# Spreading the first projections, and DVE units before V is complete, in a fused attention kernel

## The chip, the cores and the metric

The kernel runs on one core of one Trainium2 chip. The time is the device time of one execution in microseconds (us), and the median of several executions is compared. The engines are named as in the profile: PE (matmuls), PEld (weight loads, beside PE), DVE (vector work), ACT (activation functions), POOL (general purpose), SP (issues DMAs). Each engine works through its own instructions in order and waits on semaphores that the others raise.

## The reference

Two attention layers run over the same input of 2,048 tokens by 640 features, with 32 heads of 20 features. Layer A is full softmax attention; layer B attends to eight earlier tokens, two apart. A gate per token mixes them.

```python
q, k, v = qkv[0], qkv[1], qkv[2]
scores = jnp.einsum("bhqd,bhkd->bhqk", q, k) * scale      # A: every token to every token
p = _softmax(scores, axis=-1)
o = jnp.einsum("bhqk,bhkd->bhqd", p, v)                   # then reshaped and @ wo
...
idx = pos[:, None] - off[None, :]                         # B: off = 0, 2, ... 14
attn = _softmax(logits, axis=-1)
...
return g * a + (1 - g) * b                                # g = sigmoid(x . gate_w)
```

All inputs and the output are bfloat16. By far the most work is the exponential of layer A: 32 heads x 2,048 x 2,048 scores.

## The kernel before

**Units, groups and tiles.** Scores of layer A are cut into units: one head, 128 keys, 512 queries. Four heads and 512 queries make a group (`GROUPS`, L34: 4 query chunks x 8 head quads = 32 groups); a group has 16 key blocks x 4 heads = 64 units, so 2,048 in all. The order of groups starts with head quad 0 for query chunks 0 and 1, then the other seven quads of chunk 0, then those of chunk 1, and so on. Two or three units that are scored together make a tile. `next_tile` (L1463) picks them, `qk` (L1502) writes their score matmuls into one of two PSUM buffers of three banks each, and `exp` (L1535) writes one ACT instruction (L1538) over the tile, 1,024 columns for two units and 1,536 for three. The third bank of each buffer is also a bank for side work, together with one bank more, so a tile of three units needs that bank to be free.

**Units on DVE.** A tile of two units can take along a third unit, a ride, that DVE evaluates instead of ACT. DVE turns the scores into 16-bit integers whose bits, read as bfloat16, approximate the exponential (`uD`, L1528). Three shifted copies (`eD`, L797) with weighted copies of V (`vS`, on POOL, L789) smooth the approximation. So a unit on ACT costs one V-product matmul and a unit on DVE four (`pv`, L1547; matmuls at L1583). Rides are opened by `wanted` (L1389), a key block of four heads at a time, and always the last key block of a group that is still unread; an opening needs an idle DVE by the planner's reckoning. There are two thresholds: `DIDLE2` opens at any time, and the laxer `DIDLE` only once the last V block is projected and layer B's work is on schedule.

**Side work.** All else goes between the score rounds as generators in pieces: K (`gen_kd`, L582), Q (`gen_qd`) and V (`gen_v`, L717) projections, the gate, layer B (`gen_b`, `gen_bproj`), norms and the output fold (`gen_fold`). A projection piece is four matmuls of 32 columns of the array beside each other over 512 (V: 320) columns of data at L557; five pieces make a bank, which DVE then copies out. K is projected in five chunks of features, V in two halves (head quads 0 to 3, 4 to 7) of 16 key blocks. If a V product asks for a V block that is not projected yet, `run_until` (L1211) emits side work at once until it is.

**The order of work.** The kernel's Python code is itself a planner. It keeps a modelled clock per engine and appends instructions to each engine's list; the order is fixed when the program is built. After each score round and exponential, `spend` (L1614) emits side work up to a limit after the modelled end of the last exponential but one (`SLACK`), and where nothing is ready, a filler (L1590, matmuls at L1604): a matmul with no use but to keep PE working. Every parameter of these choices (`SLACK`, ride thresholds, priorities, look-ahead, filler share) is set from the table `PLAN`, keyed by the tile's number (read at L1693).

Of the kernel before, what the change touches and what calls it, by code (L numbers as in the profile page):

```python
# [21 lines left out]
KBN = S // P  # L22
# [26 lines left out]

PLAN = {  # L50
    0: ((0.34, 0.64), 0.37, 6.3, 2.5, 0.51, -1.0, -0.1, 11.8, 4.5, 7.2, 0.52, 0.47, 4.4, 1.86, 0.0, 0.85, 2, 0.0),
    10: ((0.34, 0.64), 0.37, 6.3, 2.5, -0.17, -1.0, -0.1, 13.02, 4.5, 7.2, 0.52, 0.47, 4.4, 1.86, 0.0, 0.85, 2, 0.0),
    20: ((0.34, 0.64), 0.21, 6.3, 6.6, -0.17, -1.0, -0.1, 13.02, 4.5, 8.28, 0.52, 0.47, 4.4, 1.86, 0.0, 0.85, 2, 0.0),
    30: ((0.28, 0.52), 0.35, 2.5, 6.6, 0.49, -1.55, -0.55, 9.24, 6.7, 7.2, 0.53, 0.57, 4.23, 4.64, 0.02, 0.85, 2, 1),
    50: ((0.28, 0.52), 0.35, 2.5, 6.6, 0.49, -1.55, -0.55, 9.24, 6.7, 7.2, 0.25, 0.57, 4.23, 4.64, -0.13, 0.85, 2, 1),
    60: ((0.28, 0.52), 0.35, 2.5, 6.6, 0.49, -1.55, -0.55, 9.24, 6.7, 7.2, 0.53, 0.57, 4.23, 4.28, 0.16, 0.85, 2, 1),
    70: ((0.28, 0.52), 0.1, 2.5, 6.6, 0.49, 0.2, -0.55, 9.24, 6.7, 7.2, 0.5, 0.57, 4.23, 4.64, 0.02, 0.85, 2, 1),
    80: ((0.28, 0.52), 0.34, 2.5, 5.5, 0.49, -1.55, -0.62, 9.24, 7.0, 7.2, 0.53, 0.57, 4.55, 4.64, 0.02, 0.85, 2, 1),
    90: ((0.28, 0.52), 0.3, 2.5, 6.6, 0.49, -1.55, -0.55, 9.24, 6.7, 7.8, 0.5, 0.57, 4.23, 4.64, 0.02, 0.85, 2, 1),
    110: ((0.28, 0.52), 0.3, 2.5, 6.6, 0.49, -1.55, -0.55, 8.84, 6.7, 7.8, 0.5, 0.57, 4.23, 4.64, 0.02, 0.85, 2, 0),  # L60
    120: ((0.28, 0.52), 0.3, 5.5, 6.6, 0.49, -1.34, -0.55, 8.84, 6.7, 7.8, 0.5, 0.57, 4.23, 4.64, 0.05, 0.85, 2, 0),
    130: ((0.28, 0.52), 0.19, 5.5, 6.3, 0.49, -0.24, -0.53, 9.24, 6.7, 11.3, 0.53, 0.57, 4.23, 4.93, -0.13, 0.89, 2, -3),
    140: ((0.28, 0.52), 0.3, 2.5, 2.5, 0.87, -1.55, -0.55, 8.84, 6.7, 7.8, 0.5, 0.57, 3.8, 4.64, 0.02, 0.85, 2, 0),
    170: ((0.28, 0.52), 0.3, 2.5, 2.5, 0.87, -1.28, -0.55, 8.42, 6.7, 7.8, 0.5, 0.54, 3.8, 4.64, 0.02, 0.85, 2, 0),
    180: ((0.28, 0.52), 0.39, 6.6, 2.5, 0.87, -1.55, -0.65, 10.03, 6.7, 7.8, 0.5, 0.57, 3.8, 3.83, 0.02, 0.87, 2, -3),
    190: ((0.28, 0.52), 0.19, 2.5, 2.5, 0.7, -1.55, -0.55, 7.32, 6.7, 7.8, 0.5, 0.5, 3.8, 2.96, 0.02, 0.85, 2, -3),
    200: ((0.23, 0.54), 0.35, 2.5, 2.5, 0.87, -1.55, -0.55, 7.13, 6.7, 7.71, 0.5, 0.57, 3.46, 4.13, 0.02, 0.86, 2, -3),
    210: ((0.28, 0.52), 0.3, 2.5, 2.5, 0.9, -1.55, -0.6, 7.13, 6.7, 7.71, 0.5, 0.49, 3.46, 4.64, 0.02, 0.85, 2, -3),
    220: ((0.32, 0.54), 0.3, 2.5, 2.5, 1.16, -1.55, -0.6, 7.13, 6.7, 7.71, 0.5, 0.49, 3.46, 4.64, 0.02, 0.85, 2, -3),
    230: ((0.28, 0.52), 0.3, 2.5, 2.5, 0.9, -1.55, -0.6, 7.61, 6.7, 7.71, 0.5, 0.49, 3.46, 4.64, 0.02, 0.81, 2, -3),  # L70
    250: ((0.28, 0.52), 0.3, 2.5, 2.5, 0.9, -1.48, -0.27, 7.13, 4.5, 7.32, 0.5, 0.36, 3.46, 4.64, 0.02, 0.66, 2, -3),
    280: ((0.28, 0.52), 0.3, 2.5, 2.5, 0.9, -1.48, -0.27, 7.13, 4.5, 7.32, 0.5, 0.41, 3.46, 4.64, 0.02, 0.66, 2, -3),
    290: ((0.28, 0.52), 0.3, 2.5, 5.5, 0.9, -1.6, -0.6, 7.13, 6.7, 10.69, 0.5, 0.49, 3, 4.64, 0.02, 0.67, 2, -3),
    310: ((0.28, 0.52), 0.3, 2.5, 5.5, 0.9, -1.6, -0.6, 14.73, 6.7, 10.69, 0.5, 0.49, 5.63, 4.64, 0.02, 0.67, 2, -3),
    320: ((0.28, 0.52), 0.3, 2.5, 5.5, 1.26, -1.56, -0.6, 7.13, 6.7, 10.69, 0.5, 0.53, 3, 4.64, 0.02, 0.67, 2, -3),
    330: ((0.27, 0.53), 0.26, 2.5, 5.5, 0.58, -1.6, -0.6, 7.13, 4.5, 10.54, 0.5, 0.49, 3, 4.64, 0.11, 0.67, 2, -3),
    340: ((0.27, 0.53), 0.3, 2.5, 5.5, 0.9, -1.5, -0.6, 7.13, 7.0, 10.54, 0.41, 0.49, 3.17, 4.64, 0.2, 0.67, 2, -3),
    350: ((0.27, 0.53), 0.26, 1.0, 5.5, 0.58, -1.6, -0.6, 7.13, 4.5, 10.54, 0.5, 0.49, 3, 4.64, 0.02, 0.69, 1, -3),
    360: ((0.28, 0.52), 0.37, 2.5, 5.5, 1.26, -1.56, -0.6, 7.13, 6.7, 10.69, 0.5, 0.53, 5.91, 4.64, 0.02, 0.67, 2, -3),
    400: ((0.28, 0.52), 0.37, 2.5, 5.5, 1.26, -1.56, -0.6, 7.13, 4.5, 10.69, 0.5, 0.53, 5.91, 4.64, 0.02, 0.67, 2, -3),  # L80
    410: ((0.23, 0.54), 0.22, 2.5, 6.3, 1.26, -1.56, -0.6, 7.13, 6.7, 10.69, 0.5, 0.53, 5.35, 4.64, 0.02, 0.6, 2, -3),
    420: ((0.24, 0.49), 0.3, 2.5, 5.5, 1.26, -1.56, -0.59, 7.13, 6.7, 10.69, 0.5, 0.53, 6.0, 4.64, 0.02, 0.67, 2, -3),
    430: ((0.24, 0.49), 0.3, 2.5, 5.5, 1.26, -1.56, -0.59, 7.13, 6.7, 10.69, 0.51, 0.53, 6.0, 4.64, 0.02, 0.67, 2, -3),
    450: ((0.26, 0.56), 0.3, 2.5, 5.5, 1.26, -1.56, -0.59, 7.13, 6.7, 10.69, 0.5, 0.53, 6.0, 4.64, 0.02, 0.67, 2, 0),
    480: ((0.26, 0.56), 0.3, 2.5, 5.5, 1.26, -1.4, -0.59, 9.8, 6.7, 10.69, 0.5, 0.53, 6.0, 4.64, 0.02, 0.67, 2, 0),
    500: ((0.26, 0.56), 0.3, 2.5, 5.5, 1.26, -1.56, -0.59, 7.13, 6.7, 10.69, 0.5, 0.53, 6.0, 4.64, 0.02, 0.76, 2, -1.5),
    510: ((0.26, 0.56), 0.3, 2.5, 5.5, 1.26, -1.56, -0.09, 7.13, 6.7, 10.69, 0.5, 0.53, 6.0, 4.64, 0.02, 0.76, 2, -3),
    530: ((0.21, 0.59), 0.3, 2.5, 6.6, 1.26, -1.56, -0.43, 7.13, 6.7, 10.69, 0.5, 0.53, 6.0, 4.64, -0.23, 0.76, 2, -3),
    540: ((0.21, 0.58), 0.3, 6.6, 5.5, 1.26, -0.43, -0.09, 7.13, 6.7, 10.33, 0.5, 0.53, 6.0, 4.64, 0.08, 0.76, 2, -3),
    550: ((0.21, 0.59), 0.3, 2.5, 6.6, 1.26, -1.56, -0.43, 7.13, 6.7, 11.31, 0.49, 0.53, 6.0, 4.64, -0.36, 0.76, 2, -3),  # L90
    570: ((0.2, 0.61), 0.3, 2.5, 6.6, 1.26, -1.56, -0.43, 7.13, 6.7, 10.69, 0.5, 0.53, 6.0, 4.64, -0.23, 0.76, 2, -3),
    580: ((0.2, 0.56), 0.3, 2.5, 5.5, 1.26, -1.56, 0.15, 9.66, 6.7, 8.54, 0.49, 0.48, 6.0, 4.64, -0.36, 0.76, 2, -3),
    590: ((0.2, 0.56), 0.26, 2.5, 1.0, 1.26, -1.56, 0.15, 7.13, 6.7, 11.31, 0.49, 0.31, 6.0, 4.64, -0.36, 0.76, 2, -3),
    600: ((0.28, 0.45), 0.32, 2.5, 5.5, 1.26, -0.49, -0.43, 10.79, 5.5, 10.35, 0.57, 0.53, 6.0, 4.64, -0.33, 0.66, 2, -3),
    630: ((0.28, 0.45), 0.32, 2.5, 5.5, 0.96, -0.49, -0.43, 10.79, 5.5, 10.35, 0.65, 0.53, 6.0, 4.64, -0.33, 0.66, 2, -3),
    660: ((0.28, 0.45), 0.32, 2.5, 5.5, 0.96, -0.1, -0.27, 10.79, 5.5, 10.35, 0.65, 0.53, 6.0, 4.64, -0.33, 0.66, 2, -3),
    670: ((0.28, 0.5), 0.32, 2.5, 5.5, 1.11, -0.49, -0.43, 10.79, 6.2, 10.35, 0.65, 0.55, 6.5, 4.81, -0.39, 0.62, 2, -3),
    690: ((0.3, 0.64), 0.32, 2.5, 2.5, 0.49, -1.0, -0.1, 11.8, 5.5, 7.2, 0.52, 0.47, 4.4, 4.0, 0.0, 0.85, 2, 0.0),
    700: ((0.42, 0.48), 0.32, 6.3, 5.5, 0.76, -0.49, -0.43, 10.79, 5.5, 10.35, 0.65, 0.53, 6.0, 4.64, -0.33, 0.63, 2, -3),
}  # L100
WEIGHTS = (1.0, 0.83984375, 0.70703125, 0.59375)
UOFF = 15992.765
# [217 lines left out]
def _build(ctx, nc, A_x, A_wqkv, A_wo, B_wqkv, B_wo, gate_w, out):  # L320
# [3 lines left out]
    sch = _Sched(nc, ctx)  # L324
# [242 lines left out]
    done = {}  # L567
# [13 lines left out]

    def gen_kd():  # L582
        for f in range(CN):
            m = P if f < CN - 1 else D - 4 * DH - P * (CN - 1)
            for tcc in range(4):
                b = yield from bank()
# [51 lines left out]
        done[("q", 1)] = True  # L638

    qkeys = {}  # L640
    BATCH = (0, 1, 2, 3, 4)

    def gen_qd():
# [71 lines left out]
                batch = []  # L715

    def gen_v(half):  # L717
        for kb in range(NV0 if half == 0 else 0, KBN):
            b = yield from bank()
            mms = [(side[b][:, 0:320], xT[:, c, kb * P:(kb + 1) * P],  # L720
                    kvw[:, WV_OFF + c * D + half * 320:WV_OFF + c * D + half * 320 + 320]) for c in range(CN)]
            yield from mm_group(b, mms, ["WvA"] + XT(kb // 4), mmc(320))
            yield ("dve",)
            o = _ap(vA, (kb * NQ + 4 * half) * 4 * DV + 1, [[DV, 16], [1, DH]])
            i = sap(b, 0, [[DH, 16], [1, DH]])
            t = T("dve", dvc(320), lambda e, o=o, i=i: e.tensor_copy(o, i), reads=[("side", b), "vAones"],
                  writes=[("vA", kb, half)])
            release(b, t)
            done[("v", kb, half)] = True
# [89 lines left out]
    bdone = [0.0]  # L819
# [317 lines left out]
    clock = [0.0]  # L1137
# [239 lines left out]
    DIDLE = -1.0  # L1377
    D0 = 26.0

    BT0 = 230.0  # L1380
    BT1 = 860.0
    BALL = 172.0
    DIDLE2 = -0.1
# [5 lines left out]
    def wanted(js):  # L1389
# [7 lines left out]

        if not dopen:
            if ulock[len(dquads) % 2] or len(dquads) > cur["pv"] + 1 or now < D0 or not (
                    idle >= DIDLE2 or idle >= DIDLE and done.get(("v", KBN - 1, 1)) and bdone[0] >= (now - BT0) / (BT1 - BT0) * BALL):  # L1400
                return None
            t_end = sch.avail["act"]
            for g in range(cur["g"], min(NG, cur["g"] + 2)):
# [374 lines left out]
```

## Time and profile before

| | before |
|---|---|
| device time, median of 3 | 836.64 us (835.95 to 837.18) |
| span of the profiled execution | 835.4 us |
| PE, DVE, ACT busy | 789.3, 683.7, 803.9 us |
| exponentials on ACT | 735 (479 of two units, 255 of three, 1 of one) |
| units on DVE | 324 of 2,048 |
| granted PE clock, mean | 0.998 |

A profile line of a group gives the source line, the engine, the operation, what it writes and reads, its shape and how often; then the busy time, the mean of one in nanoseconds, and the time that the engine sat idle just before, with the instruction that ended the wait. Instructions that overlap on an engine are counted once in the busy time. In a timeline line the first two numbers are the start and the length of a run of equal instructions.

### The profile page before, as it was taken

To read this page: it belongs to the slowest core of one execution; us is meant where nothing else is said; L and a number is where in the kernel's file an instruction comes from. 1 tells how busy PE (TensorE), PEld (TensorE's weight loads), DVE (VectorE), ACT (ScalarE), POOL (GpSimd) and SP (SyncE) were. 2 spreads that over 40 slices of the span, in tenths; PEclk is the share of its full clock that TensorE was granted. 3 is DMA by queue.
4 is the path that set the end of the run, shared out by engine and by line. 5 is a ranking of instruction groups with operands and counts; after the bars stand their busy time and mean duration, and the time that the engine had idled before them with its cause. 6 is when DMAs were issued, how large, how long until landed. Compare 5 with 4: busy or idle time off the path is not lost.

```text
span 835.4 us, 29602 instructions
## 1 busy us (share of the span) xinstructions
PE 789.3 (94%) x12599; PEld 289.9 (35%) x12601; DVE 683.7 (82%) x1205; ACT 803.9 (96%) x767; POOL 138.7 (17%) x180
## 2 busy tenths in 40 slices
PE   8999999999999899989998999999999999998997
PEld 4333323334333332333233333333333333333223
DVE  7567888889888887978797988798898898887873
ACT  4999999999999999999999999999999999999994
POOL 5013013431111111011111011111102111101110
PEclk9999999999999999999999999999999999999999
DMA  9112112200111110011001011110011001101100
GB/s 313 30 37 44 33 25 45 73 13 19 29 37 29 29 30 20 7 42 32 20 18 41 18 20 29 36 42 9 5 39 30 10 20 25 38 6 31 32 6 34
DMA packets 45016, 29.15 MB, mean 35 GB/s; under 512 B 27204, under 2 KB 43684, under 8 KB 44884
## 3 DMA queue, kind: packets, MB, share of 16 engines
q1 hardware_dynamic: 44596, 26.92, 12.4%
q8 instruction: 100, 1.64, 0.8%
q10 hardware_dynamic: 288, 0.33, 0.1%
q14 instruction: 32, 0.26, 0.1%
HBM read 11.94 MB, written 2.62 MB: 17 GB/s over the span
## 4 chain that ended last, share of the span: by engine, by line
PE 54%; ACT 30%; issue 10%; DVE 5%; DVEq 0%; ACTq 0%
ACT ebuf L1538 30%; PE score L1515 17%; PE obank L1583 13%; PE side L557 13%; PE score L557 5%; PE obank L1604 2%; DVE uD L1528 1%; PE side L1604 1%; DVE eD L797 1%; PE obank L459 1%; PE score L1230 1%; PE side L885 1%; DVE stage L869 0%; PE score L1604 0%; DVE stage L970 0%
## 5 line engine op out<-in xcount | busy, mean ns | idle before, releaser
L1538 ACT ACTIVATE ebuf<-score 128x1024 bf16<-128x1024 f32 (+1 forms) x735 | 792.6, 1237 | 11.6 <-PE score L1515 9.7
L1515 PE MATMUL score<-qT,kT 32*128 32x512 bf16 x2048 | 291.9, 384 | 31.6 <-ACT ebuf L1538 20.6
L1528 DVE TENSOR_SCALAR uD<-score 128x512 int16<-128x512 f32 x324 | 217.2, 683 | 38.4 <-PE score L1515 36.1
L797 DVE TENSOR_SCALAR eD<-uD 128x2048 int16<-128x2048 int16 x243 | 168.1, 722 | 7.9 <-PE obank L1583 7.2
L1515 PEld LDWEIGHTS score<-qT,kT 32*128 32x128 bf16 x2048 | 75.1, 91 | 282.7 <-ACT ebuf L1538 137.6
L1583 PE MATMUL obank<-ebuf,vA 128*21 128x512 bf16 x1724 | 161.3, 385 | 2.2 <-ACT ebuf L1538 1.8
L789 POOL TENSOR_TENSOR vS<-vA,vw 128x252 bf16<-128x252 bf16 x81 | 61.0, 757 | 291.5 <-PE obank L1583 256.3
L557 PE MATMUL side<-xT,kvw 128*32 128x256 bf16 (+1 forms) x2530 | 103.0, 281 | 3.1 <-DVE qkvB L853 1.4
L1583 PE MATMUL obank<-eD,vS 128*21 128x512 bf16 x972 | 84.1, 382 | 0.0
L557 PEld LDWEIGHTS side<-xT,kvw 128*32 128x32 bf16 x2530 | 59.3, 96 | 37.9 <-issue 22.0
L764 POOL TENSOR_TENSOR rcp<-rcp,gA 128x16 f32<-128x16 f32 x31 | 11.3, 365 | 351.9 <-DVE rcp L762 351.9
L1583 PEld LDWEIGHTS obank<-ebuf,vA 128*21 128x21 bf16 x1724 | 38.6, 89 | 82.3 <-issue 69.5
L970 DVE TENSOR_TENSOR stage<-qkvB,repB 128x1280 bf16<-128x1280 bf16 x64 | 52.9, 856 | 0.7 <-DMA repB<-eB 0.7
L869 DVE TENSOR_TENSOR stage<-qkvB 128x1280 bf16<-128x1280 bf16 x64 | 51.4, 830 | 0.1
L853 DVE CAST qkvB<-side 128x512 bf16<-128x512 f32 (+1 forms) x72 | 41.9, 591 | 10.5 <-PE side L557 10.5
L557 PE MATMUL side<-stage,ident 128*32 128x512 bf16 (+1 forms) x736 | 47.4, 345 | 1.2 <-DVE uD L744 0.5
L1604 PE MATMUL obank<-xT,zero 128*32 128x512 bf16 x444 | 37.9, 385 | 0.0
L770 POOL TENSOR_TENSOR oN<-oTt,rcp 128x512 bf16<-128x512 f32 x31 | 33.0, 1065 | 2.4
L1583 PE MATMUL obank<-uD,vA 128*21 128x512 bf16 x324 | 31.7, 382 | 0.0
L758 DVE STREAM_TRANSPOSE oTt<-obank 128x512 f32<-128x512 f32 x32 | 22.7, 709 | 9.0 <-PE obank L1583 8.9
L1583 PEld LDWEIGHTS obank<-eD,vS 128*21 128x21 bf16 x972 | 24.0, 92 | 17.4 <-issue 4.1
L557 PE MATMUL side<-woA_d,oTd 128*32 128x128 bf16 (+1 forms) x580 | 28.8, 293 | 0.0
(173 smaller groups left out, 555.5 us busy)
## 6 DMA issues: line engine op xcount, KB each, us to landing
repB<-eB SPq DMA_DIRECT2D x128, 32.0 KB
WqP<-in_A_wqkv_dram SPq DMA_DIRECT2D x16, 160.0 KB
stage<-in_B_wqkv_dram SPq DMA_DIRECT2D x1, 2400.0 KB
oTd<-oN SPq DMA_DIRECT2D x108, 20.0 KB
qT<-dst SPq DMA_DIRECT2D x104, 20.0 KB
out_dram<-outsb SPq DMA_DIRECT2D x12, 160.0 KB
kvw<-in_A_wqkv_dram SPq DMA_DIRECT2D x2, 800.0 KB
oTd<-in_A_x_dram SPq DMA_DIRECT2D x2, 640.0 KB
```

The lines of the kernel that those rows point to most:

```text
L557: ins = e.matmul(o[j:k, :], l(j) if callable(l) else l[:, j:k], r, start=(first and i == 0), stop=(last and i == n - 1), skip_group_check= ...
L770: T(en, c2, lambda e: e.tensor_tensor(oo, ii, ib, ALU.mult), reads=["rcp", "oTt"], writes=["oN0"])
L789: T("pool", 0.7, lambda e: e.tensor_tensor(vS[:, d % 2, :, :], _ap(vA, (kb * NQ + q) * 4 * DV, [[0, K - 1], [1, 4 * DV]]), _ap(vw, 0, [[1, ...
L797: T("dve", 0.11 + 0.1334 * n, lambda e, k=k, sl=sl: e.tensor_scalar(eD[:, sl % NS, 0:512 * n].bitcast(I16), uD[d % 2][:, 0:512 * n].bitcas ...
L853: t = TB(dvc(n * TOK), lambda e, o=o, i=i: e.tensor_copy(o, i), reads=[("side", b)], writes=[key])
L869: TB(dvc(CN * TOK, 2), lambda e, w=w, ks=ks: e.tensor_tensor(prodB(w), qB[:, :, :], ks, ALU.mult), reads=["qB", "kB"], writes=[("prod", w) ...
L970: TB(dvc(CN * TOK, 2), lambda e, w=w, vs=vs, rr=rr: e.tensor_tensor(prodB(w), vs, rr, ALU.mult), reads=["vB", ("repB", w4 % NR)], writes=[ ...
L1515: ins = e.matmul(o, kT[32 * j:32 * j + 32, q, kb * P:(kb + 1) * P], qT[g % NQT][32 * j:32 * j + 32, :], start=True, stop=True)
L1528: t = T("dve", 0.69, lambda e: e.tensor_scalar(uD[d % 2][:, 512 * i:512 * (i + 1)].bitcast(I16), side[x], UOFF, 0.0, op0=ALU.add, op1=ALU. ...
L1538: exps[s] = T("act", actc(512 * n), lambda e: e.activation(ebuf[s % NE][:, 0:512 * n], score[s % 2][:, 0:512 * n], ACTF.Exp, scale=LN2 / S ...
L1583: ins = e.matmul(obank[32 * j:32 * j + DV, :], v, src, start=(kb == 0), stop=(last and k >= len(lst) - 4), skip_group_check=True)
L1604: ins = e.matmul(o[32 * j:32 * j + 32, :], w[:, 32 * j:32 * j + 32] if best else w[:, :], xT[:, 0, 0:512], start=bool(best), stop=bool(bes ...
```

## The change

Three edits. First, the K chunks 2, 3 and 4 may not start before 78, 98 and 120 us of the planner's clock (`KT`), and the second half of V not before 70 (`VT`). Q follows, since a query chunk waits for its K chunk. What was emitted as early as priorities allowed is to be spread over the first groups. Second, the condition that the last V block be done is dropped from the laxer ride threshold, so DVE can take units while late V blocks are missing. Third, the whole table `PLAN` is replaced by one with other values and other tile numbers.

```diff
 PLAN = {
     0: ((0.34, 0.64), 0.37, 6.3, 2.5, 0.51, -1.0, -0.1, 11.8, 4.5, 7.2, 0.52, 0.47, 4.4, 1.86, 0.0, 0.85, 2, 0.0),
-    10: ((0.34, 0.64), 0.37, 6.3, 2.5, -0.17, -1.0, -0.1, 13.02, 4.5, 7.2, 0.52, 0.47, 4.4, 1.86, 0.0, 0.85, 2, 0.0),
-    20: ((0.34, 0.64), 0.21, 6.3, 6.6, -0.17, -1.0, -0.1, 13.02, 4.5, 8.28, 0.52, 0.47, 4.4, 1.86, 0.0, 0.85, 2, 0.0),
-    30: ((0.28, 0.52), 0.35, 2.5, 6.6, 0.49, -1.55, -0.55, 9.24, 6.7, 7.2, 0.53, 0.57, 4.23, 4.64, 0.02, 0.85, 2, 1),
...
+    20: ((0.34, 0.64), 0.37, 1.0, 2.5, 0.51, -1.0, 0.3, 11.8, 4.5, 7.2, 0.52, 0.47, 4.4, 2.53, 0.0, 0.84, 3, 0),
+    30: ((0.3, 0.64), 0.31, 1.0, 2.5, 0.49, -1.6, -0.1, 11.8, 7.0, 8.15, 0.52, 0.47, 4.4, 4.0, 0.0, 0.71, 2, 0.0),
+    50: ((0.34, 0.64), 0.37, 1.0, 2.5, 0.51, -1.0, 0.04, 10.92, 4.5, 7.09, 0.52, 0.36, 4.4, 1.86, 0.07, 0.85, 2, -1.5),
...
     def gen_kd():
         for f in range(CN):
+            while max(sch.avail["pe"], clock[0]) < KT[f]:
+                yield ("cond",)
             m = P if f < CN - 1 else D - 4 * DH - P * (CN - 1)
...
+    KT = (0.0, 0.0, 78.0, 98.0, 120.0)
+    VT = 70.0
...
     def gen_v(half):
+        while half and max(sch.avail["pe"], clock[0]) < VT:
+            yield ("cond",)
         for kb in range(NV0 if half == 0 else 0, KBN):
...
             if ulock[len(dquads) % 2] or len(dquads) > cur["pv"] + 1 or now < D0 or not (
-                    idle >= DIDLE2 or idle >= DIDLE and done.get(("v", KBN - 1, 1)) and bdone[0] >= (now - BT0) / (BT1 - BT0) * BALL):
+                    idle >= DIDLE2 or idle >= DIDLE and bdone[0] >= (now - BT0) / (BT1 - BT0) * BALL):
                 return None
```

The 18 values of a row set, in this order: `SLACK`, `XTOL`, `XPRIO`, `XLATE`, `DWAIT`, `DIDLE`, `DIDLE2`, `DTIME`, `DLOW`, `DLATE`, `DVE_AHEAD`, `DAHEAD`, `BOOST`, `XBOOST`, `RFILL`, `FILL`, `HOLD`, `BOFF`.

## The prediction

> **What bounds the kernel now.** I read the page's engine shares first, then ACT by form of instruction, then all engines in two stretches, then the waits, and last single stretches of the timeline.
>
> ```profile
> PE 789.3 (94%) x12599; PEld 289.9 (35%) x12601; DVE 683.7 (82%) x1205; ACT 803.9 (96%) x767; POOL 138.7 (17%) x180
> ...
> PE 54%; ACT 30%; issue 10%; DVE 5%; DVEq 0%; ACTq 0%
> ```
>
> ACT is busiest, yet the chain that ended last runs through PE for 54%. Two engines bound this kernel in turn, so the next view is by stretch (columns: span, then PE, PEld, DVE, ACT, POOL busy).
>
> ```profile
> 19.60:150.40 130.80, 129.91 (x1836) 42.41 (x1840) 97.89 (x187) 127.46 (x130) 24.83 (x27) 1.00 0.17 38
> 150.40:823.80 673.40, 635.38 (x10474) 234.62 (x10462) 566.50 (x975) 667.20 (x627) 101.62 (x132) 1.00 0.10 26
> ```
>
> From the first exponential (19.6 us) to 150.4, where the projections of K, Q and V are all but done, PE is busy 129.9 of 130.8 us: PE is the bound, and ACT loses about 3 us. After it ACT is: 667.2 of 673.4, PE 94%.
>
> ```profile
> L1538 ACT ACTIVATE ebuf<-score 128x1024 bf16<-128x1024 f32 x479 | 463.4, 1082 | 6.4 <-PE score L1515 5.0
> L1538 ACT ACTIVATE ebuf<-score 128x1536 bf16<-128x1536 f32 x255 | 359.2, 1530 | 5.1 <-PE score L1515 4.4 <-ACT ebuf L1538 0.2
> ...
> 202.83 13.60 ACT L1538 ACTIVATE ebuf<-score 128x1536 bf16<-128x1536 f32 x10
> ```
>
> Successive exponentials overlap, so their price is start to start. Ten three-unit tiles take 13.6 us with the last one's overlap: 1.330 each. The starts of two-unit tiles are 0.904 apart in the median. By these prices 479 and 255 tiles and one single (0.5) take 772.7, other work of ACT in between 5.1 (eight eB at 0.477, eight tB at 0.104, four gates at 0.12), and the first exponential's start to the last one's end is 804.2. So 26 us are lost in small waits, more than the 11.6 shown as idle, since a delay under the overlap shows as a longer instruction.
>
> ```profile
> 203.81 0.94 PE L557 MATMUL side<-xT,kvw 128*32 128x256 bf16 x28
> 204.68 0.39 PE L1515 MATMUL score<-qT,kT 32*128 32x512 bf16 x3
> 205.00 0.51 PE L557 MATMUL side<-xT,kvw 128*32 128x256 bf16 x12
> 205.34 0.60 PE L1604 MATMUL obank<-xT,zero 128*32 128x512 bf16 x8
> 205.87 0.39 PE L1515 MATMUL score<-qT,kT 32*128 32x512 bf16 x3
> 206.19 0.61 PE L1583 MATMUL obank<-ebuf,vA 128*21 128x512 bf16 x8
> 206.63 0.40 PE L557 MATMUL side<-xT,kvw 128*32 128x256 bf16 x8
> ```
>
> These starts price PE. A score round (two or three 32-row matmuls beside each other) goes from 205.87 to 206.19: 0.32. Eight 21-column matmuls of 512 take 0.44, so four take about 0.216. The eight before the round at 205.87 take 0.53, 0.1 more, so a round costs 0.32 + 0.1 = 0.43 whether it feeds two units or three. A projection piece of 512 and a filler are four matmuls, 0.216; a V piece of 320 columns 0.135; one of 128 0.056 (rows of 20: 0.28).
>
> **What the skill says.** *TensorEngine Tiling (Array Packing)*, Key Properties: changing the tiling mode drains TensorE. The trace agrees: 0.1 us on either side of a round. *ScalarE: Activation LUTs*, What ACT_TABLE_LOAD costs: 186 ns + 0.833 ns per column, with 93 ns overlap, an estimate of 946 and 1,373 ns here. The trace has 904 and 1,330: the step of 512 columns agrees, the fixed part is 43 ns less; I use the trace. *TensorE: Matmul & The Clock Gate*, What's actually happening: about 3.4 us of idleness halves the clock. Here one dip shows, granted clock 0.91 over 440 to 460, after PE fell to 16.5 of 20 us busy.
>
> **The change, part by part.** The plan table sets which instructions exist, so I counted the changed kernel's instruction order.
>
> *Units.* 2,048 score units are split between ACT and DVE. DVE takes 318 instead of 324, in spite of the relaxed condition: six more on ACT. Its tiles are 401 of two and 309 of three, for 479 and 255. ACT: 401 x 0.904 + 309 x 1.330 + 0.5 = 774.0, against 772.7: +1.3. DVE sheds 6 x (0.683 + 3 x 0.722/4), 7 us, worth nothing at 82% busy. PE has 24 score rounds less (-10.3), but 79 fillers more (266 for 187, +17.1). K, Q, V, gate and B projections are as many as before: 514 pieces of 512, 155 of 320.
>
> *Projections and the first stretch (PE-bound).* Before, 309 units are started at tile 127 (150.3 us); PE's work to there is 127 rounds 54.6, 99 fours of the V product 21.4, 141 pieces of 512 30.5, 127 of 320 17.1, 14 fillers 3.0, five query bounds (rows of 128) 0.6: 127.2, and took 130.7. In the changed kernel 309 units are started at tile 120: 120 rounds 51.6, 21.4, the same 141 pieces 30.5, 140 of 320 18.9, 21 fillers 4.5, 0.6: 127.5. So the spreading moves projections within the stretch, not out of it; with the same 3% on top +0.3. ACT needs 123.3 and 122.9 there, so PE stays the bound.
>
> *A new wait.* DVE units take the last key block of a group first. Allowing one before V is complete makes the V product at tile 24 ask for block 15, and the planner then emits 19 V pieces (2.6 us) between two score rounds; before, tile 24 has two. The backlog is counted above, but behind the last piece the V product also waits for its copy on DVE (L726, 0.49), and the score rounds stand behind it on PE. Bounds: 0 (copies done early) and 0.9 (a copy and two handovers); I take 0.5. Deferring K chunks 2 to 4 adds no wait: they stand at tiles 55 to 105, and the first group that reads chunk 2 starts near tile 125.
>
> *The rest (ACT-bound).* Before: 372 x 0.904 + 235 x 1.330 + 0.5 + 4.9 = 654.3 in 673.5 us, so 19.2 lost; summing starts by form, 15.4 behind two-unit tiles (41 ns each), 3.3 behind three-unit ones (14 ns), where PE has longer for side work. After: 315 and 275 tiles, 284.8 + 365.8 + 5.4 = 656.0, +1.7. At these rates the loss is 13.0 + 3.9, -1.8. The 72 fillers more in this part (+15.6) I cost at nothing: in the old trace tiles with a filler lose 21 ns, those without 33, so fillers fall into holes.
>
> *Tail.* After the last exponential PE still works off the output fold. Behind the last V product stand 21 pieces of 128 instead of 14: +0.4, on the path, since ACT and DVE wait for PE there.
>
> Sum: 836.6 + 0.3 + 0.5 + 1.7 - 1.8 + 0.4 = 837.7, no change within 0.2%.
>
> **Rivals.** *Faster, about 831.* Fewer rounds leave real PE work in the second part 10 us lower, and three-unit tiles give slack. The best 40 us of the old trace (200 to 240, half the tiles three-unit) lose 0.2 us. If the 16.9 falls to 11, and the dip at 440 to 460 (stretch loss 2.6, typical 1) doesn't recur, 837.7 - 5.9 - 1.0 = 831. For it: the changed kernel has more such tiles everywhere. Against: of the 19.2, 12.6 stand behind tiles where a V product is the last thing ahead of the next score round, and the costly ones among these (two-unit tiles with three or more fours) are 36 before and 34 after.
>
> *Slower, about 842.* The wait at tile 24 takes its upper bound (0.9 for 0.5: +0.4), and a quarter of the added fillers' 15.6 (3.9) comes in front of a score round that is already late. 837.7 + 0.4 + 3.9 = 842. For it: PE is 94% busy and fillers are fixed in its order. Against: the fillers' record.
>
> *ACT takes only its instruction count,* 24 fixed costs less with nothing else moving: 24 x 0.05 makes 835.5 and is inside "no change".
>
> **Chances and range.** No change 0.37 (both same-side cases), faster 0.34, slower 0.29: the computed shift is 1.1 us of a 26 us store of losses whose rearrangement I can't follow tile by tile. Range 829.5 to 843.5: it takes in the faster and slower cases, and the wait's bounds.
>
> **What would show it.** ACT: 401 and 309 exponentials, about 774 at the prices. PE still over 99% busy to tile 120, reached near 151 us. One ACT wait of 2 to 3 us near 45 to 50 us, behind V pieces at L559. Waits of ACT on scores in the second part near those of before. Wrong if the loss behind two-unit tiles leaves 41 ns by a third either way, if clock dips are more or fewer, or if PE's first stretch shortens, which would mean that the order, not the amount, sets it.

## The result, and the profile after

| | before | after |
|---|---|---|
| device time, median of 4 | 836.91 us (835.95 to 837.58) | 842.54 us (lowest 840.53) |
| ratio to before, 95% interval | | 1.006, 1.0036 to 1.0084 |
| the same kernel once more | | 842.57 us (842.02 to 843.34, 5 runs): 1.0065, 1.0045 to 1.0084 |
| span of the profiled execution | 835.4 us | 841.1 us |
| exponentials of two / three units | 479 / 255 | 401 / 309 |
| units on DVE | 324 | 318 |

The changed kernel is slower by 5.6 us by the medians, 0.6% to 0.7%. One of its four executions, the profiled one, was disturbed (1,358 us, with PE busy for 1,343.8), so the ratio leaves it out and the trace read here is that of the repeat. The other three and the five of the repeat have a median of 842.5 too. In the changed kernel's file the same code stands 2 to 8 lines lower: L1546 is L1538 of the kernel before, L559 is L557.

The page of the changed kernel, engine shares and the chain that ended last:

```profile
span 841.1 us, 30105 instructions
...
PE 795.7 (95%) x12897; PEld 294.5 (35%) x12899; DVE 677.1 (81%) x1196; ACT 804.3 (96%) x743; POOL 132.3 (16%) x179
...
ACT 45%; PE 40%; issue 11%; DVE 2%; DMA 1%; SPq 0%; DVEq 0%; ACTq 0%
```

ACT is as busy as before (804.3 for 803.9), and PE as the page counts it only 6.4 us busier. Yet 5.7 us were added to the span, so the shares don't tell where. The next view cuts the span at the first exponential, at the tile that comes nearest to 200 started units (84 before, 74 after), at 309 units (tiles 127 and 120) and at the end of the last exponential. Columns as in the prediction. Before:

```profile
19.62:106.05 86.43, 86.18 (x1267) 29.03 (x1266) 61.00 (x126) 83.61 (x86) 12.49 (x14) 1.00 0.17 42
106.05:150.31 44.26, 43.62 (x573) 13.29 (x569) 36.89 (x62) 43.76 (x44) 12.34 (x13) 1.00 0.15 31
150.31:823.80 673.49, 635.47 (x10474) 234.70 (x10466) 566.50 (x975) 667.28 (x627) 101.62 (x132) 1.00 0.10 26
```

After:

```profile
18.94:106.14 87.20, 84.12 (x1269) 28.46 (x1269) 66.21 (x133) 81.10 (x76) 13.05 (x15) 1.00 0.19 48
106.14:152.67 46.53, 45.85 (x652) 15.42 (x647) 31.91 (x59) 45.29 (x47) 12.65 (x12) 1.00 0.13 25
152.67:827.70 675.03, 641.48 (x10664) 237.73 (x10652) 560.28 (x963) 668.67 (x610) 94.35 (x131) 1.00 0.10 26
```

Each stretch is set against the prices of its exponentials, start to start (0.904 and 1.330 us). The price is what ACT needs for them; the loss is what is left of the stretch when ACT's other work is taken off too (0.24 in the stretch to 200 units, 5.5 in the last). So it holds every delay, also one that hides under an overlap.

| stretch | price before, after | loss before, after | longer by |
|---|---|---|---|
| to the first exponential | | | -0.7 |
| to 200 units | 81.05, 78.82 | 5.14, 8.14 | +0.8 |
| 200 to 309 units | 42.28, 44.14 | 1.98, 2.39 | +2.3 |
| 309 units to the last exponential | 648.8, 650.5 | 19.17, 19.02 | +1.5 |
| last exponential to the end | | | +1.8 |

These sum to +5.7. The first 309 units take 3.0 us longer, and that is all loss (+3.4), while their price is 0.4 lower: DVE takes 25 units of the first 200 (20 before) and 10 of the next 109 (15 before), which moves two microseconds of ACT's work from the one stretch into the other.

The waits of ACT on scores in the first stretch, 19.6 to 150.3 us of the kernel before, tell the same (columns: us in total, times, longest):

```profile
ACT ebuf L1538 <- PE score L1515: 4.9, 7, 2.1
```

In the changed kernel, 19 to 152.7:

```profile
ACT ebuf L1546 <- PE score L1523: 9.4, 11, 3.2
```

The longest of these is at tile 24, shown by the timeline of the changed kernel (start, length, engine; in brackets the idle time before and its releaser):

```profile
43.42 0.39 PE L1523 MATMUL score<-qT,kT 32*128 32x512 bf16 x2
43.74 0.73 PE L559 MATMUL score<-kvw,xT 128*32 128x320 bf16 x16
44.29 0.85 PE L559 MATMUL side<-kvw,xT 128*32 128x320 bf16 x20
44.97 1.53 PE L559 MATMUL score<-kvw,xT 128*32 128x320 bf16 x40
...
46.56 0.49 DVE L734 CAST vA<-score 128x320 bf16<-128x320 f32 x1 [0.19 <-PE score L559]
...
47.10 0.40 PE L1591 MATMUL obank<-ebuf,vA 128*21 128x512 bf16 x4 [0.60 <-DVE vA L734]
...
47.65 0.61 PE L1523 MATMUL score<-qT,kT 32*128 32x512 bf16 x6
48.15 2.37 ACT L1546 ACTIVATE ebuf<-score 128x1536 bf16<-128x1536 f32 x2 [3.19 <-PE score L1523]
```

Between the score round at 43.42 and that at 47.65 stand 19 V pieces (76 matmuls in three lines), the copy of the last block on DVE, and the V product that waits 0.60 us for it. ACT is idle for 3.19 us. This wait was forecast. The next one, at tiles 57 to 59, was not:

```profile
85.70 0.45 DVE L780 STREAM_TRANSPOSE oN<-oN 128x256 f32<-128x256 f32 x1 [1.67 <-DMA oTd<-oN]
86.07 0.65 DVE L1536 TENSOR_SCALAR uD<-score 128x512 int16<-128x512 f32 x1
...
86.78 0.61 PE L1612 MATMUL score<-xT,ident 128*32 128x512 bf16 x8 [0.99 <-DVE uD L1536]
...
87.32 0.60 PE L1523 MATMUL score<-qT,kT 32*128 32x512 bf16 x3
...
88.02 1.02 ACT L1546 ACTIVATE ebuf<-score 128x1024 bf16<-128x1024 f32 x1 [0.92 <-PE score L1523]
```

Read from the bottom: ACT waits for scores; the score round is queued behind a *filler* (L1612), work without use; the filler waits 0.99 us for its bank, which DVE has to empty (`uD`); and DVE stood 1.67 us at a transpose that waits for a DMA. Tiles 57 to 59 lose 1.9 us. Each engine works in order, so a wait of one DVE instruction for a transfer came through two queues to ACT. The start of this chain is the late transfer. Its last two packets of 1 KB start at 84.6 and 84.7 us, all others by 83.7, and a 16 KB instruction fetch of 1.36 us starts at 83.2. The run with the padded end (below), whose first part is unedited, shows the same once more: a fetch, the last two packets 0.9 us behind the others, 1.8 us of DVE's wait, 2.0 us lost at tiles 57 to 59. In four more traces of this order, with an edit in the first part (no early fillers, thin fillers, the two with the burst thinned), all packets start by 83.6, no fetch starts before the last of them, and DVE waits 0.6 us or not at all. That the fetch holds the transfer up fits the six traces, but no run moves the fetch alone.

The end of both traces, first the last ACT instruction with its wait and the last issue of an output transfer before:

```profile
830.75 1.08 ACT L1082 ACTIVATE stage<-score 128x512 bf16<-128x512 f32 x2 [6.93 <-PE score L1063]
...
832.11 0.96 SPq L1090 DMA_DIRECT2D out_dram<-stage  x2
```

and after:

```profile
835.26 0.60 ACT L1090 ACTIVATE stage<-side 128x512 bf16<-128x512 f32 x1 [7.55 <-PE side L1071]
...
836.63 0.96 SPq L1098 DMA_DIRECT2D out_dram<-stage  x2
```

ACT waits 0.6 us longer for PE's fold, which the prediction put at 0.4 for the whole tail. From the last issue to the end it is 835.4 - 832.1 = 3.3 before and 841.1 - 836.6 = 4.5 after: 1.2 us that no instruction of an engine shows.

### The profile page after: what moved, and what is told of

It reads as the page before. It is cut to its first block, busy times and chain, and to the rows that moved or that the text cites. A ratio compares the mean times of both kernels' runs of the same rounds, so it can differ in the third digit from the quotient of the medians.

```text
span 1356.3 us, 30107 instructions
## 1 busy us (share of the span) xinstructions
PE 1343.8 (99%) x12899; PEld 375.2 (28%) x12899; DVE 690.5 (51%) x1196; ACT 864.8 (64%) x743; POOL 129.0 (10%) x179
## 3 DMA queue, kind: packets, MB, share of 16 engines
q8 instruction: 102, 1.67, 0.5%
## 4 chain that ended last, share of the span: by engine, by line
PE 99%; DVE 1%; ACT 0%; issue 0%; DVEq 0%; ACTq 0%
PE side L559 29%; PE obank L1591 26%; PE score L1523 25%; PE score L559 5%; PE obank L1612 5%; PE score L1612 2%; PE side L1612 2%; PE side L893 1%; PE score L1238 1%; PE obank L461 0%; PE obank L1261 0%; PE side L1261 0%; ACT ebuf L1546 0%; PE side L690 0%; PE side L919 0%; PE side L940 0%
## 5 line engine op out<-in xcount | busy, mean ns | idle before, releaser
L1546 ACT ACTIVATE ebuf<-score 128x1024 bf16<-128x1024 f32 (+1 forms) x711 | 851.1, 1208 | 450.4 <-PE score L1523 449.3
L1523 PE MATMUL score<-qT,kT 32*128 32x512 bf16 x2048 | 398.0, 539 | 1.4 <-ACT ebuf L1546 0.8
L1591 PE MATMUL obank<-ebuf,vA 128*21 128x512 bf16 x1730 | 230.2, 549 | 0.9 <-DVE vA L734 0.6
L559 PE MATMUL side<-xT,kvw 128*32 128x256 bf16 (+2 forms) x2710 | 205.4, 443 | 0.8 <-DVE dst L667 0.4
L805 DVE TENSOR_SCALAR eD<-uD 128x2048 int16<-128x2048 int16 (+1 forms) x240 | 162.9, 702 | 15.9 <-PE obank L1591 15.0
L1591 PE MATMUL obank<-eD,vS 128*21 128x512 bf16 x954 | 155.3, 673 | 0.0
L559 PEld LDWEIGHTS side<-xT,kvw 128*32 128x32 bf16 (+1 forms) x2710 | 87.4, 124 | 86.4 <-issue 57.9
L559 PE MATMUL side<-stage,ident 128*32 128x512 bf16 (+1 forms) x768 | 84.7, 560 | 1.2 <-DVE oB L995 0.7
L1612 PE MATMUL obank<-xT,zero 128*32 128x512 bf16 x536 | 74.5, 628 | 0.0
L559 PE MATMUL side<-woA_d,oTd 128*32 128x512 bf16 (+1 forms) x520 | 49.2, 492 | 0.0
L559 PE MATMUL side<-woBp,oB 128*32 128x512 bf16 (+1 forms) x520 | 45.1, 484 | 0.4 <-DVE qkvB L861 0.4
L1612 PE MATMUL score<-xT,ident 128*32 128x512 bf16 x276 | 44.5, 663 | 0.0
L559 PE MATMUL side<-xT,WqP 128*32 128x512 bf16 x320 | 41.5, 641 | 0.0
```

The lines of the kernel that those rows point to most:

```text
L559: ins = e.matmul(o[j:k, :], l(j) if callable(l) else l[:, j:k], r, start=(first and i == 0), stop=(last and i == n - 1), skip_group_check= ...
L805: T("dve", 0.11 + 0.1334 * n, lambda e, k=k, sl=sl: e.tensor_scalar(eD[:, sl % NS, 0:512 * n].bitcast(I16), uD[d % 2][:, 0:512 * n].bitcas ...
L1523: ins = e.matmul(o, kT[32 * j:32 * j + 32, q, kb * P:(kb + 1) * P], qT[g % NQT][32 * j:32 * j + 32, :], start=True, stop=True)
L1546: exps[s] = T("act", actc(512 * n), lambda e: e.activation(ebuf[s % NE][:, 0:512 * n], score[s % 2][:, 0:512 * n], ACTF.Exp, scale=LN2 / S ...
L1591: ins = e.matmul(obank[32 * j:32 * j + DV, :], v, src, start=(kb == 0), stop=(last and k >= len(lst) - 4), skip_group_check=True)
L1612: ins = e.matmul(o[32 * j:32 * j + 32, :], w[:, 32 * j:32 * j + 32] if best else w[:, :], xT[:, 0, 0:512], start=bool(best), stop=bool(bes ...
```

## The experiments

**The kernel again.** No edit; it gives the trace above and the scale of what repeats.

> The changed kernel unaltered, for an undisturbed trace. If the forecast's terms were right in kind, the first stretch (to the start of tile 120) lasts about 131 to 134 us instead of 130.7, with one ACT wait of 2 to 3 us near tile 24, and the rest loses about 17 us behind exponentials. Theory A (score rounds come late: PE order): the 5 to 6 us more are lost behind exponentials whose next score round follows a long PE stretch. Theory B (added fillers): the loss stands behind tiles with a filler. Theory C (more clock dips): the granted clock shows more half-speed stretches than the one of before. Time 842, ratio 1.006.

Measured: 842.57 us, as said. The slowdown is the kernel's own.

**Fillers of the first stretch left out, in both kernels.** The prediction read PE as the bound to 309 units. If so, PE work taken away there must come off the time. All fillers before tile 120 (21 of them, 4.5 us) and before tile 127 in the old kernel (14, 3.0 us) are struck from PE's list after planning; the rest keeps its order, and their waits go to the next PE instruction that writes the same bank.

```diff
+    CUT = 120                      # 127 in the kernel before
...
+        if len(tiles) <= CUT:
+            dropped.append((t, key))
...
+    sch.drop(dropped)
     sch.emit()
```

> The changed kernel in the same order, with the 21 fillers before tile 120 taken out (the waits that they did for a bank pass to the next instruction that writes it). Theory A (PE is the bound of the first stretch, so all that stands on it there counts): 21 x 0.216 = 4.5 us off, and up to 1.0 for a filler that waited for DVE at tile 57: 842.6 - 4.5 to 5.5 = 837 to 838. Theory B (the first stretch is set by the order of exponentials and score rounds, not by PE's amount of work): 842, no change. A clock dip in the first stretch would hide it.

> The kernel before in the same order without the 14 fillers before tile 127. Theory A: 14 x 0.216 = 3.0 us off, 833.6. Theory B: 836.6.

Measured: after 842.82 us (841.26 to 845.34; ratio 1.0078, 1.0063 to 1.0093), before 836.87 (1.0002, 0.9994 to 1.0011). Neither moves. In its trace the changed kernel's way to 309 units is 131.8 us instead of 133.7, nearly all of it in the first 200 units (loss 6.30 for 8.14). Of these 1.8 us, 1.5 are at tiles 57 to 59, where 0.4 is lost instead of 1.9. That doesn't price the filler: DVE doesn't wait for its transfer here, and with thin fillers (below), where the filler is still in its place, the three tiles lose 0.3. From 200 to 309 units the loss is 2.29 for 2.39, and the kernel before gains 0.6 to 309 units (130.1 for 130.7) of 3.0 us of work. Without the fillers PE is busy for this much of the first 200 units:

```profile
18.97:104.33 85.36, 81.47 (x1205) 26.98 (x1205) 66.18 (x134) 80.81 (x76) 13.17 (x15) 1.00 0.20 49
```

95%, with 4 us free, and the stretch is shorter mainly by what a *wait* cost. So PE's amount was not the bound; most of the fillers filled PE's holes here as well. *Perfetto Trace Analysis*, Identifying the Most-Contended Engine, says that matmul busy share is no good measure of how close PE is to its limit, since pipelined matmuls look smaller in the trace. This run agrees with the conclusion, though by another way, work without use: of "129.9 of 130.8 us busy", 3 us in the kernel before could go for nothing. The profiled execution gained 1.4 us in all (839.7 for 841.1), but the median of six didn't, so even the 1.8 us are not shown to be worth anything in the time. Part of the spread is PE's clock: the two of the six at a granted clock of 0.999 took 841.3 and 841.6 us, the four at 0.994 to 0.997 took 842.5 to 845.3, while the five of the unedited kernel are at 0.997 to 0.999.

**The V burst thinned, alone and without the early fillers.** The V blocks that the planner emits in one go at tile 24 keep their instructions at the ends, but of the five input chunks three are all but left out and the last works on 64 of 320 columns, so V is incomplete here and only the time counts.

```diff
+            cut = len(tiles) == 25 and n == 5 and not callable(mms[0][1]) and mms[0][2].shape[-1] == 320
...
+                        if cut and 0 < i < n - 1 and j < n_ - 32:
+                            continue
```

> The changed kernel in the same order, with the projection of the last V blocks of the first half between the score rounds of tiles 24 and 25 cut short (three of five input chunks are left out for those four blocks, so their V is incomplete), which takes about 1.8 us of PE out of the burst. Theory A (ACT's wait of 3.2 us at tile 24 is lost for good): the wait falls to about 1.4, the first stretch from 133.7 to about 132, and the end comes 1.8 earlier, 840.8. Rival (later slack takes it up, since PE has more to do than ACT over the whole stretch anyway): the wait falls, but tile 120 starts as late as before, 842.6.

> As the run before, and without the 21 fillers before tile 120, one of which stood behind a DVE queue that waited for a transfer. Theory A: the first stretch about 130, as in the kernel before, and the time 839; what is then left against the kernel before, 2.5 us, is the second part (+1.5) and the end. If the time is 842 all the same, the loss of the first stretch is given back later and the cause lies in the second part.

Measured: 842.08 us (839.87 to 844.43; 1.0056, 1.0034 to 1.0077) and 841.57 (840.35 to 842.88; 1.0053, 1.0036 to 1.0069). ACT's longest wait is still there with most of the PE work in it gone:

```profile
ACT ebuf L1550 <- PE score L1527: 14.3, 24, 2.5
```

The loss of tile 24 falls from 3.33 to 2.69 only. In this trace four copies of V blocks stand on DVE one behind the other, PE waits 0.43 us for a bank that the first of them empties and then 0.76 for the last, so the copies now set the length of the wait; no run takes them out. Tile 57 loses nothing here, since DVE waits 0.6 us for the transfer instead of 1.7, and the way to 309 units is 132.0 us, 1.7 shorter. With both edits it is 132.1: the two gains are largely the same wait and don't add. The medians are 0.5 and 1.0 us below the unedited kernel's, inside the spread of the runs. At equal granted clock both edits together come out lower: 840.4 at 0.998 and 841.5 to 842.1 at 0.997, where the repeat has 842.6 and 842.9, and 843.3. That is 1.3 to 2.6 us, from few runs. In the second trace a dip of PE's clock to half at 268 us (6.8 us long) costs 2.8 at three tiles, and behind tile 120 21.4 us are lost instead of 19.0; in that of the burst alone 20.5, so that the last exponential ends only 0.2 us earlier than unedited.

**The parts alone.** First the deferral of K and V with the old table, then the new table with the old code:

```diff
     def gen_kd():
         for f in range(CN):
+            while max(sch.avail["pe"], clock[0]) < KT[f]:
+                yield ("cond",)
```

> The kernel before with the late starts of K chunks and V half alone; old plan table, old condition. Its order has 304 units on DVE and tiles of 551 and 214. Prices of the forecast: ACT 782.7 against 772.7 is +10, losses behind tiles +2 to 3, PE to 309 units 130.2 for 128.1: 848 to 850. If spreading by itself helped, it would stay near 837 in spite of the units.

> The new plan table alone, in the old code without late starts and with the old ride condition. Its order has 296 units on DVE and 367 and 339 tiles: ACT's prices 783.1, +10.5 to the kernel before, losses as in it or 1 to 2 less, so 845 to 848. If the table by itself carried the gain and the late starts only cost, it would be below 842.

Measured: 873.65 us (1.0464, 1.0432 to 1.0496) and 872.24 (1.0412, 1.0388 to 1.0436): each part alone costs 35 to 37 us, together they cost 5.6. ACT's prices explain 10 of that (782.7 and 783.1 for 772.7: 304 and 296 units on DVE instead of 324). For the rest, the waits of the deferral alone:

```profile
ACT ebuf L1544 <- PE score L1521: 24.0, 45, 2.1
ACT stage L1088 <- PE side L1069: 19.6, 1, 19.6
```

This trace is of the slowest of four executions (881.1 us). Its last exponential ends at 854.2 of 879.3 us: 25 us of tail, with ACT waiting for side work that the old table, made for other tile numbers, left for the end. The new table with the old code shows a tail of 18.4 and waits up to 5.0 us. The third part has no run: the old table with the relaxed condition alone gives the old order instruction for instruction, and with all three code edits the order of the deferral alone. So the relaxed condition does nothing by itself with the old table; and what a part is worth can't be read by taking it alone, since the table fits one code only.

**DVE's V products not ahead of V.** The burst comes from a DVE unit whose V product asks for a block that isn't projected. Here the planner waits with that product until the block is there:

```diff
+            if not done.get(("v", dquads[d][1], GROUPS[pvg][1] // 4)) and not (force and end_g):
+                break
             ok = done.get(("ds", d, k))
```

> The changed kernel with one line more in the planner: a DVE unit's V product is not taken before its V block is projected, so the burst at tile 24 is not asked for. The rest is planned anew: 300 units on DVE, 386 and 325 tiles, ACT's prices 781.7 (+7.7). By the prices 842.6 + 7.7 - 2 to 3 for the wait = 847 to 848. If the burst was the main cause, it would be 838 or below.

Measured: 867.97 us (1.0369, 1.0346 to 1.0391). The edit replans everything behind it (300 units on DVE, prices 781.7), and a larger wait takes the burst's place (7.2 us at tile 32). It doesn't price the burst; it shows again how far a local edit moves the plan.

**Thin fillers and thin side work.** To see what PE's amount is worth with the order kept, fillers were cut from 512 to 64 columns; then, in both kernels, all but the first piece of every side product (four of a projection's five) were cut to 64 columns, which leaves the products incomplete.

```diff
-  ... o[32 * j:32 * j + 32, :], ..., xT[:, 0, 0:512], ...
+  ... o[32 * j:32 * j + 32, 0:64], ..., xT[:, 0, 0:64], ...
```

```diff
-  e.matmul(o[j:k, :], l(j) if callable(l) else l[:, j:k], r, ...
+  e.matmul(o[j:k, 0:64] if i else o[j:k, :], l(j) if callable(l) else l[:, j:k], r[:, 0:64] if i else r, ...
```

> The changed kernel in the same order, each filler 64 columns wide instead of 512, so 266 fillers cost PE about 12 us less in all. Theory B (fillers delay score rounds): about 838 or less. Theory A: 841 to 843, no change. Theory C: the clock dips more often, 843 or more.

> The changed kernel in the same order, with four of five pieces of every side product (projections, layer B, fold) cut to 64 columns, so those products are not complete. PE is relieved of some 100 us. Theory A: ACT is then the only bound, losses behind exponentials fall to a few us: 19.6 + 774.0 + 5.1 + about 8 of tail = 807 to 815, and 1 to 2 us above the kernel before cut the same way. If the gap to that one stays at 5 us, PE lateness is not the cause.

> The kernel before with the same cut of the side products (four of five pieces at 64 columns, those products not complete). Theory A: 805 to 813, 1 to 2 us below the changed kernel cut the same way (ACT's own work is 772.7 against 774.0).

Measured: 851.75 us (1.0172, 1.0137 to 1.0208), 854.44 (1.02, 1.0148 to 1.0252) and 857.57 (1.025, 1.0209 to 1.0291). Less work on PE makes the kernel slower by 9 us with the fillers and by 12 and 21 with the side work. In the traces this goes with PE's clock. Two dips with thin fillers, each with the 3.4 us ahead of it (columns as in the prediction: the span, the busy times from PE on, then the granted clock, DMA share and GB/s):

```profile
751.80:755.20 3.40, 2.44 (x52) 0.98 (x48) 2.60 (x8) 3.40 (x4) 0.00 (x0) 1.00 0.02 5
755.20:762.00 6.80, 6.80 (x85) 2.10 (x85) 4.35 (x8) 6.20 (x8) 1.54 (x3) 0.50 0.09 25
779.10:782.50 3.40, 2.41 (x52) 0.88 (x49) 3.16 (x6) 3.40 (x4) 0.00 (x0) 1.00 0.03 8
782.50:789.30 6.80, 5.54 (x55) 1.28 (x55) 3.88 (x8) 5.02 (x6) 1.72 (x2) 0.50 0.01 2
```

The same two stretches ahead, in the changed kernel with its full fillers:

```profile
751.80:755.20 3.40, 3.21 (x45) 0.99 (x41) 2.34 (x8) 3.40 (x4) 0.00 (x0) 1.00 0.02 5
779.10:782.50 3.40, 3.40 (x48) 0.93 (x49) 2.85 (x5) 3.02 (x4) 0.00 (x0) 1.00 0.02 5
```

With thin fillers PE is busy for 2.4 of these 3.4 us, and the clock then falls to half for 6.8; with full ones it is busy for 3.2 and 3.4 about there, and nothing falls. The trace has seven dips, where the changed kernel itself has one of 3.4 (at 588 us, 1.1 us lost at tile 498). The mean clock is 0.981, and 0.916 and 0.925 with thin side work, against 0.998. The traces let the two be told apart. To the last exponential the loss is 34.1 us with thin fillers, 29.6 with full ones (the trace is of the fastest of its four executions; its span is 4.5 us longer). At the tiles in and just behind dips it is 9.5 for 1.2; at all others 24.7 for 28.4. So the dips cost 8.3 us more, and thinning the fillers saved 3.8 elsewhere, 2.0 of it before 309 units, most of that at tiles 57 to 59. By this account the time as a whole prices the clock, and without the dips less filler work would have been a small gain. PE's busy time fell by 27.4 us (768.3 for 795.7), more than twice the 12 us expected.

**The end padded.** If code at the end of ACT's and DVE's streams had to be fetched in the last microseconds, more instructions there would lengthen the gap behind the last transfer. Waits already fulfilled were added in front of the tail's last work (50 instructions on ACT, 18 on DVE).

```diff
+                        if t is self.pad.get(sname):
+                            for _ in range(PAD[sname]):
+                                eng.wait_ge(*max(waited.items(), key=lambda x: x[1]))
```

> The changed kernel with 50 and 18 empty wait instructions more on ACT and DVE in the idle time of the tail, which gives both engines the instruction counts of the kernel before. In the traces the changed kernel needs 4.5 us from its last output transfer's issue to the end, the one before 3.3; two instruction fetches stand in that time instead of one. Theory D (a fetch at the program's end meets the last transfers, which depends on the instruction counts): this gap falls to about 3.3 and the time to about 841.4. Otherwise the gap stays at 4.5 and the time at 842.6.

Measured: 846.81 us (1.0126, 1.0111 to 1.014). But the waits hold up ACT itself: its wait ahead of the output copy is 11.7 us instead of 7.5 and ends by its own issue:

```profile
ACT stage L1096 <- issue: 11.7, 1, 11.7
```

That 4.2 is as much as the time grew (846.8 for 842.6), so the time can't tell what the gap waits for. The gap itself did shrink. ACT's queue now issues the last output transfer, behind SP's:

```profile
841.49 0.86 ACTq L1105 DMA_DIRECT2D out_dram<-stage  x2
```

From there to the end it is 844.7 - 841.5 = 3.2 us instead of 4.5, as expected, and one instruction fetch stands in that time, as in the kernel before, instead of two. But the edit also changed which queue issues last.

## Where the prediction held and where it failed

The forecast was no change, 837.7; the time is 842.5, within the range of 829.5 to 843.5. That it lies inside is owed to the width of the range: the sum is 4.8 us off, and three of its four terms missed by 1.4 us and more. By its own terms:

| term | forecast | trace |
|---|---|---|
| first stretch and new wait | +0.8 | +3.0, less 0.7 for an earlier start |
| prices on ACT, rest | +1.7 | +1.7 |
| loss behind tiles, rest | -1.8 | -0.15 |
| tail | +0.4 | +1.8 |

**First stretch: the step that failed is its bound.** "PE is the bound" was read from PE's 129.9 busy of 130.8 us, and so the two stretches were costed by amounts of PE work, +0.3. The runs without early fillers show that the amount isn't what sets it. Its own sign failed too: PE is busy for 130.0 of 133.7 us (97%), not over 99%. What sets the stretch is ACT's price and its waits for score rounds that stand behind other work in PE's order: the price fell by 0.4 and the loss rose by 3.4. The clue was in the old profile: ACT was busy 127.5 of 130.8, and "ACT needs 123.3" was dismissed beside PE's number. In the two traces with the first part unedited the way to 309 units is 133.7 and 134.9 us (the second loses 1.0 at tile 3 besides); in the four with an edit there it is 131.7 to 132.1. At tiles 57 to 59 these four lose 0.3 to 0.8 us instead of 1.9, so 1.1 to 1.6 of the 3.0 us go with the late transfer there, which a small shift in time makes punctual.

**The new wait: the mechanism was right, its size was not.** One ACT wait of 2 to 3 us behind V pieces at L559 came (3.19 us, at 48 us, the V product waiting 0.60 for the copy against a forecast 0.5). But with PE as the bound, the 19 V pieces were "counted above" and only the copy was added. With ACT as the bound the wait itself counts, 3.3 us, less what it replaces (tile 33, 1.1 before). Its cause was also misread: with the old table the relaxed condition moves nothing, and planned with the old condition the new kernel asks for the same late V block at the same tile. The new table's first rows keep `DTIME` at 11.8 where the old row 10 has 13.02, and that puts DVE's first units at tile 14 into the first group, whose late V blocks are missing: by the planner's clock that group's exponentials end 12.7 us later, more than 11.8 and less than 13.02. This is read from the rows and the planned order, not from a run.

**Fillers.** In the second part they cost little, as forecast: tiles with a filler lose 24 ns (21 before), those without 35 (34). Since fillers go where nothing else is ready, these are different places, and the better measure is the thin fillers: outside the dips they save at most 1.8 us there, while PE's busy time in the whole kernel falls by 27.4 us (768.3 for 795.7). In the first part one filler of 21 stood in a chain that cost 1.9 us: it waited for a bank and the score round was behind it. The prediction costed fillers by their duration and not by what they wait for; but the late transfer started this chain, and no run shows what the filler added to it.

**Loss behind tiles.** The forecast carried 41 and 14 ns over to the new counts. Two-unit tiles lose 50 ns now (15.8/315), less than a third away from 41, three-unit ones 12 (3.2/275). The heavy two-unit tiles, with three or more fours of the V product (four matmuls each) last ahead of the next score round, are 36 before and 34 after and lose 178 and 195 ns each: 6.4 and 6.6 us. The others are 55 fewer and lose 9.0 and 9.2 us. Either those that went had lost next to nothing, or the ones that stayed lose more; the traces don't tell which. The prediction had the count of heavy tiles and used it only against its faster rival, while its own sum took a class average over to a changed mix.

**Tail.** The fold was right in size (+0.6 for +0.4). The 1.2 us between the last transfer's issue and the end was not in the sum. In the traces of the changed order, the padded one apart, the gap is 4.3 to 4.5 us, and 3.8 with both cuts, with two instruction fetches in it; in those of the old order it is 3.3 with one. DVE's products held back give 3.3 (one), the new table alone 3.9 (two), the padded end 3.2 (one). The deferral alone doesn't fit: 4.2 with one. That is a correlation with one exception; what the gap waits for stays open.

**The rivals.** "Slower, about 842" hit the number by other means: the wait took more than its upper bound, and its 3.9 us of fillers late in the second part didn't come. "Faster" needed a loss of 11 us in the last part and no dip of the clock; it got 19.0 and a dip in another place.

What stays open: how much of the slowdown the wait at tile 24 is, since the cut of its PE work shortened it by 0.6 us only; whether the 1.7 to 1.9 us of the first stretch that three edited kernels save in the trace are worth as much in the time, since their medians differ from the unedited one's by less than the runs spread; what made the transfer at tile 57 late; and the gap at the end.

## What to carry to other kernels

A busy share of 99% doesn't make an engine the bound where part of its work is filler, or where its instructions stand in line behind waits: sum the prices of both engines, and where neither makes up the length of the stretch, follow what ends the *waits*. Cost an added instruction by what it waits for and what is queued behind it. Before a wait is put down to an instruction that stands in it, look at the same place in other traces of that order. Where an edit changes the clock, count the loss at the dips apart from the rest. And when counts of a class change, ask which members of the class go: an average loss need not hold for a changed mix.

## What the runs showed of the hardware

Taking useless work from PE slows this kernel. With fillers of 64 instead of 512 columns, in the same places, PE is 91% busy instead of 95% and the median is 9 us higher; in the trace, of the fastest execution, the clock falls to half for 3.4 or 6.8 us at seven places, and the span is 4.5 us longer. *TensorE: Matmul & The Clock Gate*, What's actually happening, has the clock fall to half after an idle window of about 3.4 us. The steps of 3.4 us agree. But "idle" needs no standstill: ahead of each of the seven dips, and of the one in either unedited kernel, PE was busy for 1.5 to 2.6 of the 3.4 us. Stretches of 3.4 us with PE busy for less than 2.5 make up 2.0% of all placements in the kernel before, 2.4% in the changed one and 6.4% with thin fillers.

The dips begin on a grid. In the traces of all runs but the disturbed execution, 59 dips stand between 20 us and the last exponential, and each begins a whole number of steps of 3.413 us after the trace's first clock record (132 steps in the kernel before, 171 in the changed one). PE was busy for 25% to 86% of the step ahead. Of the changed kernel's steps at full clock five lie under 75%, and only the lowest, at 61%, is followed by a dip; with thin fillers 19 do, and six are. So the share of time that PE is busy doesn't decide alone, and these traces give no threshold. Leaving out 21 fillers in the first 150 us, between dense projections, brought no dip in its profiled execution; the lower clocks of four others say that dips can have come there. A filler can be worth something where a thinner PE would let the clock fall, and here it cost little elsewhere.
